# Attention beside a Fourier product on one core: the turned rows' transfers on ACT's queue, PV bursts of 6, 6 and 4 chunks, and stage two's half products added straight from PSUM by VectorE

## The chip, the cores and the metric

One core of a Trainium2 chip runs the whole program. The metric is the device time of one execution in microseconds (us); lower is better. A measurement of this kernel is the median over several executions, and one further execution is recorded by the hardware profiler. The engines are TensorE (PE; its weight loads are PEld), VectorE (DVE), ScalarE (ACT), GpSimd (POOL) and SyncE (SP), which here only issues transfers (DMAs).

## The reference

Two independent results stand side by side in the output, the left 1024 columns from attention and the right 1024 from a Fourier mix:

```python
# A: 2048 x 1024 input, 32 heads of 32 columns, one shared key and value head
q = (x @ wq).reshape(1, 2048, 32, 32).transpose(0, 2, 1, 3)
k, v = x @ wk, x @ wv
p = softmax(einsum("bhqd,bkd->bhqk", q, k) * 32 ** -0.5)
a = einsum("bhqk,bkd->bhqd", p, v)  ->  (2048, 1024) @ wo
# B: real part of a two-dimensional Fourier transform of another 2048 x 1024 input
ar = einsum("bsd,ed->bse", xb, hid_re);  ai = einsum("bsd,ed->bse", xb, hid_im)
b = einsum("ts,bse->bte", seq_re, ar) - einsum("ts,bse->bte", seq_im, ai)
out = concatenate([a, b], axis=-1)
```

## The kernel before

**Two streams on TensorE.** The first stream is attention: 32 units (a block `b` of 512 queries times a group `g` of 4 heads), each of 32 steps. A step `n` makes one scores block of 128 queries by 1024 keys (`scores`, L592, tile `pss`, two buffers in PSUM), from which VectorE takes the row maximum into `nm` (`TENSOR_REDUCE nm<-pss`) and ScalarE, one step later, the exponentials' sums (`row_sums`, L603). The same step makes, for the unit before, one block of transposed scores (`expo`, L655, tile `pst`, one buffer of two banks), whose exponentials ScalarE writes to a tile `p` (13 of these exist). Scores run 44 steps ahead of `expo` (`SU + LEAD`, 32 + 12).

The second stream is the **fill**: all other matrix products, cut into groups that add up in one PSUM bank (`psb`, two banks in all): keys, values and queries, then **stage one** and **stage two** of the Fourier mix, then the output product with `wo`. Each product is computed as three products of split operands (hi and lo: `rh`, `rl` on the right, `mh`, `ml` on the left; hi by hi, hi by lo, lo by hi), so a group of 8 right tiles has 24 matrix instructions, which this text calls 24 fills. `level` (L745) spreads the fills evenly over the steps, about five a step, and `take` (L341) issues them. `pos["fill"]` counts them, and everything that prepares operands is timed by that count.

**PV bursts.** At three steps of each unit (`ENDS`, twice the entries of `CUT`, L664: here steps 12, 22 and 32) `pv` (L666) multiplies the finished `p` tiles by the values `v`: one burst of 6, 5 and 5 chunks of 128 keys. A burst uses the psb bank that the open group does not use; `aside` (L367) first issues up to 6 fills so that a group is never within 6 fills of its start or end when a bank is borrowed. No fills are issued in a step that ends in a burst.

**Turned rows.** When all scores of a unit are done, `lse_1`, `lse_1b` and `lse_2` make, from the maxima and sums, three rows of numbers per query block. `lse_3` (L634) turns them by a transposition on TensorE into a borrowed psb bank, and VectorE copies the result to the tile `mt`. `lse_4` (L643) sends `mt` away in three transfers of 8 KB: two into rows 96 and 97 of the unit's query tile `qst`, where `expo` of that unit reads them, and one to `r_d` in DRAM. `TURN` and `LSE` (L714, L715) set the steps: counted from the first step after the unit's last scores, `lse_1` in step 1, `lse_1b` in 2, `lse_2` in 4, `lse_3` in 6, `lse_4` in 8. Step 12 of that count is the first `expo` of the unit.

**Operands of the fill.** Right operands (`RL`) and left ones (`ML`) go through four stages each: load by SP's queue into a staging tile (`r`, three buffers for the first source and two for the second; `m` likewise), `comb` (L200), which adds or subtracts the sources on GpSimd, the hi `cast` (L174, on GpSimd after the start), and `lo`, a subtraction on GpSimd. An operand is due by a fill count; a right one is loaded and combined 40 fills ahead of that, cast 14 ahead, and its lo made 8 ahead. SP issues all loads and stores of the program in one order, and a load into a staging tile waits there until GpSimd has read the tile's last contents.

**Stage two.** Seven products (`PRODUCTS`, a scheme of Strassen's kind) of 16 right tiles and 8 row blocks `k` each. The 16 right tiles make two halves of 8, so a product is two sets of 8 groups with 24 fills. Lefts of products 1, 2, 4, 5 and 6 are sums of two sources, rights of 1, 3, 5, 6 and 7 too. Each product goes to one or two output blocks `y(t, e, k)`. In the first half VectorE copies a group's bank to a tile `qh` and it is stored to `hs` in DRAM. In the second half `hs` is loaded again, VectorE adds the bank to it, and GpSimd adds that joined block to each output block that exists already (64 additions in all); a first contribution is stored as it is. Blocks that a group needs are loaded into one of six `y` tiles 24 fills before the group ends, and stored 9 fills after it ends (`BEHIND`).

Of the kernel before, what the change touches and what calls it, by code (L numbers as in the profile page):

```python
# [8 lines left out]
F32 = mybir.dt.float32  # L9
F32R = mybir.dt.float32r  # L10
AF = mybir.ActivationFunctionType
# [5 lines left out]
P = 128  # L17
S = 2048
D = 1024
H = 32  # L20
DH = 32
W = 512
# [65 lines left out]
def tile_kernel(ctx: ExitStack, tc, xT, wq, wkv, wo, xbT, wT, cT, out):  # L88
# [44 lines left out]
    def move(q, to, of):  # L133
        q.dma_start(to.bitcast(F32), of.bitcast(F32))
# [34 lines left out]
                k = next(k for k in (3, 2, 1, 0) if self.may(k))  # L169
                self.step(k)  # L170

    pos = {"fill": 0, "s": 0}

    def cast(to, of):  # L174
        if pos["fill"] < START:
            act.activation(to, of, AF.Copy)
        else:
            gp.tensor_copy(to, of)
# [19 lines left out]
            sp.dma_start(it.t[-1], a)  # L198

    def comb(it):  # L200
        if it.pre:
            return
        for t, (_, sg) in zip(it.t[1:], it.srcs[1:]):
            (gp.tensor_add if sg > 0 else gp.tensor_sub)(it.t[0], it.t[0], t)
        if it.raw is not None:
            store(it.raw[0], it.t[0], it.raw[1])
# [69 lines left out]

    prev = {"set": -200, "this": 0}
    end = [0]

    def pump():  # L280
        RL.pump()
# [25 lines left out]
    def store(to, of, key=None):  # L307
        def go():
            move(sp, to, of)
            if key:  # L310
                ready.add(key)
        soon(go)
# [28 lines left out]
    def take(n):  # L341
        for _ in range(n):
            if cur["group"] >= len(groups):
                return
            g = groups[cur["group"]]
            j = pos["fill"] - g.at
            if j == 0:
                cur["ps"] = bank("psb", True)
            if j % 3 == 0:
                RL.force(g.right[j // 3])  # L350
            if j % 12 == 0:
                ML.force(g.left[j // 12])
            product(g, cur["ps"], j)
            pos["fill"] += 1
            if j == g.n - 1:
                cur["group"] += 1
                assert all(hasattr(it, "done") for it in g.ys)
                g.post(cur["ps"])
                cur["at"] += 1
                used[cur["bank"]] = cur["at"]  # L360
                cur["bank"] = None
                if g.ys:
                    at(pos["fill"] + 2 * BEHIND, lambda n=len(g.ys): yused.__setitem__(0, yused[0] + n))
            pump()
            run_later()
# [106 lines left out]
    def have(key, ap):  # L472
        assert key in ready, key
        return ap

    def stage2():
        seen, total = {}, {}
        for _, _, outs in PRODUCTS:
            for t, e, _ in outs:
                total[t, e] = total.get((t, e), 0) + 1  # L480
        for f, (mt, nt, outs) in enumerate(PRODUCTS):
            hs = [dram.tile([P, W], F32, name=f"hs_{f}_{k}") for k in range(8)]
            for half in range(2):
                R = [Item([(lambda s=s, k=k: have((k, s), s_d[k][s]), -1 if nt == SUB and i else 1) for i, k in enumerate(nt)])
                     for s in range(half * 8, half * 8 + 8)]
                for k in range(8):
                    left = []
                    for q in range(2):
                        s0 = half * 8 + q * 4
                        left.append(Item([(lambda a=a, k=k, s0=s0: cT[a[0], a[1] * 8 + k, :, s0:s0 + 4], a[2]) for a in mt]))  # L490
                    if half == 0:
                        def post(ps, k=k, hs=hs, f=f):
                            o = op.tile([P, W], F32, name="qh")
                            dve.tensor_copy(o, ps)
                            store(hs[k], o, ("h", f, k))
                        yield Group(left, R, post)
                        continue
                    part = Item([(lambda k=k, hs=hs, f=f: have(("h", f, k), hs[k]), 1)])
                    ys = [part]
                    plan = []  # L500
                    for t, e, sg in outs:
                        n = seen.get((t, e, k), 0)
                        seen[t, e, k] = n + 1
                        it = None
                        if n:
                            it = Item([(lambda t=t, e=e, k=k: y_d[t][e][k], 1)])
                            ys.append(it)
                        r0 = (t * 8 + k) * P
                        to = out[r0:r0 + P, D + e * W:D + (e + 1) * W] if n + 1 == total[t, e] else y_d[t][e][k]
                        plan.append((sg, it, to))  # L510

                    def post(ps, part=part, plan=plan):
                        h = part.y
                        dve.tensor_add(h, h, ps)
                        for sg, it, to in plan:
                            if it is not None:
                                (gp.tensor_add if sg > 0 else gp.tensor_sub)(it.y, it.y, h)
                                store(to, it.y)
                            elif sg > 0:
                                store(to, h)  # L520
                            else:
                                o = op.tile([P, W], F32, name="qh")
                                act.activation(o, h, AF.Copy, scale=-1.0)
                                store(to, o)
                    yield Group(left, R, post, ys=ys)


# [115 lines left out]
    def lse_4(u):  # L643
        mt = lse.pop(u)
        for a in range(2):
            move(sp, qst[u][96 + a:97 + a].rearrange("o h (t c) -> o (h t) c", c=P), mt[a * NC:(a + 1) * NC])
        sp.dma_start(r_d[u], mt[2 * NC:])

    def inverse(u):
        rb[u] = onp.tile([P, W], F32, name="rb")  # L650
# [10 lines left out]
            te.matmul(ps[:, a], kst[:, c * P:(c + 1) * P], qst[u][:, 2 * hp_ + a], start=True, stop=True)  # L661
        act.activation(pt[u, c, hp_], ps, AF.Exp)

    CUT = (0, 6, 11, NC)  # L664

    def pv(u, k):  # L666

        aside()
        ps = bank("psb")
        for c in range(CUT[k], CUT[k + 1]):  # L670
            for h in range(4):
                te.matmul(ps[h * DH:(h + 1) * DH], v[:, c], pt[u, c, h // 2][:, h % 2], start=c == CUT[k], stop=c == CUT[k + 1] - 1)
        if k == 0:
            ov[u] = onp.tile([P, W], F32, name="ov")
            dve.tensor_copy(ov[u], ps)
        else:
            dve.tensor_add(ov[u], ov[u], ps)
        cur["at"] += 1
        if k == len(CUT) - 2:
            b, g = units[u]  # L680
            hi_ = onp.tile([P, W], F32R, name="oh")
            lo_ = onp.tile([P, W], F32R, name="ol")
            lse["out"] = hi_, lo_

            last = u + 1 == len(units)
            e = dve if last else gp

            def low():
                e.tensor_sub(lo_, ov[u], hi_.bitcast(F32))
                if not last:  # L690
                    store(oh_d[b][g], hi_)
                    store(ol_d[b][g], lo_, ("o", b, g))

            ends.append(lambda: e.tensor_mul(ov[u], ov[u], rb[u]))
            ends.append(lambda: e.tensor_copy(hi_, ov[u]))
            ends.append(low)

    def score_step(s):

        if s < total:  # L700
            u, r = divmod(s, SU)
            if r == SU - 6 and u + 1 < len(units):
                open_unit(u + 1)
        if SU <= s < SU * (len(units) + 1) and s % SU == TURN:
            lse_3((s - SU) // SU)
        if s < total:
            scores(s)
        row_sums(s - 1)
        u, e = divmod(s - SU, SU)
        if 0 <= u < len(units):  # L710
            for f in LSE.get(e, ()):
                f(u)

    TURN = 6  # L714
    LSE = {1: (lse_1,), 2: (lse_1b,), 4: (lse_2,), 8: (lse_4,)}  # L715

    room = [(lambda t=t, k=k: t[:, k]) for t in [pp.tile([P, 2, W], F32, name="p") for _ in range(NP)] for k in range(2)]
    for n, (it, to) in enumerate(zip(RL.items, room)):
# [7 lines left out]
    take(66)  # L726
    for s in range(SU + LEAD):
        score_step(s)
        take(7)

    PRO = pos["fill"]
# [13 lines left out]
    def level(n):  # L745
        r = n % SU
        if r in ENDS:
            return
        more = min(e for e in ENDS if e > r) - r
        left = goal(n + more) - pos["fill"]  # L750
        take(left - left * (more - 1) // more)

    for n in range(total):
        u, r = divmod(n, SU)
        if n == total - 12:
            w1 = wo_set(1)
            add([o_group(NQ - 1, t, e, ws) for e, ws in ((0, w0), (1, w1)) for t in range(4)])
        score_step(n + SU + LEAD)
        if ends:
            ends.pop(0)()  # L760
        expo(n)
        if r == 16:
            inverse(u)
        if r in ENDS and n:
            pv((n - 1) // SU, (ENDS.index(r) - 1) % (len(CUT) - 1))
        level(n)


# [70 lines left out]
```

## Time and profile before

| | us |
|---|---|
| median of 3 runs (lowest, highest) | 2813.01 (2805.11, 2813.58) |
| the profiled execution | 2811.13 |
| its span on the core | 2809.3 |
| PE busy | 2767.0 |
| ACT busy | 2176.8 |
| DVE busy | 1601.6 |
| POOL busy | 1598.2 |

The profiled execution's own time has 1.8 us outside the span. In the trace all of the kernel's own instructions carry line 66, the helper that records them, so they are told apart by their tiles' names: `out<-in`. Buffer numbers are left out, so all the `psb` banks have one name. SPq is SP's queue, which issues transfers. PE is busy nearly throughout, but its instructions are pipelined, and a busy PE can be a slow one: the granted clock stands beside it in the tables by stretch.

Counted by its matrix instructions, the fill reaches stage one at about 350 us, stage two at 1054 us and the output product at 2498 us. The halves of stage two's products begin at 1054, 1156, 1253, 1355, 1463, 1566, 1662, 1763, 1879, 1982, 2078, 2182, 2293 and 2396 us.

### The profile page before, as it was taken

The page shows a single profiled execution, that of the slowest core. Times are in us where ns is not written, and L with a number is a line of the kernel's source. Part 1 is how long each engine was busy: PE and PEld are TensorE (multiplying, and loading weights), DVE is VectorE, ACT ScalarE, POOL GpSimd, SP SyncE. Part 2 cuts the span into 40 slices and gives each one's busy share as a digit, 9 for nine tenths or more (in the row PEclk, how much of TensorE's full clock was granted, in tenths as well). Part 3 has the DMA queues.
Part 4 walks back from the last instruction along what each step waited for, and adds up shares of the span by engine and source line. Part 5 has one row for each costly group of instructions (what it writes and reads, how often), then busy time and mean ns, then how long its engine had stood idle before and what let it go on. Part 6 is the DMA issues. An engine that isn't in the chain of part 4 may idle for free.

```text
span 2809.3 us, 40359 instructions
## 1 busy us (share of the span) xinstructions
PE 2767.0 (98%) x13904; PEld 1936.5 (69%) x13904; DVE 1601.6 (57%) x1832; ACT 2176.8 (77%) x3151; POOL 1598.2 (57%) x1593
## 2 busy tenths in 40 slices
PE   8999999999999999999999999999999999999999
PEld 5876676676766766767666676667666667767666
DVE  6766666666666665555555555555555556556401
ACT  4578787888878888888878888878888778888740
POOL 3754524565536447766675575797787775540110
PEclk9999999999999999999999999999999999999999
DMA  7643325675676555665554464665565553554455
GB/s 257 196 147 113 125 87 188 218 240 181 214 241 207 165 161 186 185 184 149 167 193 133 150 188 140 195 211 173 186 201 169 177 185 105 169 175 150 123 168 170
DMA packets 320449, 489.73 MB, mean 174 GB/s; under 512 B 33978, under 2 KB 99002, under 8 KB 320186
## 3 DMA queue, kind: packets, MB, share of 16 engines
q1 hardware_dynamic: 320244, 487.15, 55.2%
q8 instruction: 110, 1.80, 0.3%
q14 instruction: 95, 0.78, 0.1%
HBM read 366.22 MB, written 119.28 MB: 173 GB/s over the span
## 4 chain that ended last, share of the span: by engine, by line
PE 89%; DMA 5%; POOL 2%; issue 2%; SPq 1%; ACT 1%; DVE 1%; POOLq 0%; ACTq 0%; DVEq 0%
PE psb L66 56%; PE pss L66 17%; PE pst L66 16%; DMA r<-s 2%; SPq L66 1%; POOL ml L66 1%; DMA qst<-mt 1%; POOL mh L66 0%; DMA p<-in_xT_dram 0%; ACT pss L66 0%; DMA m<-in_cT_dram 0%; POOL rh L66 0%; DMA r<-in_xT_dram 0%; ACT p L66 0%; DMA ql<-ql 0%
## 5 line engine op out<-in xcount | busy, mean ns | idle before, releaser
L66 DVE TENSOR_REDUCE nm<-pss 128x1 f32<-128x1024 f32 x1024 | 1252.6, 1223 | 594.6 <-PE pss L66 594.0
L66 ACT ACTIVATE p<-pst 128x1024 f32<-128x1024 f32 x1024 | 1053.4, 1029 | 487.2 <-PE pst L66 485.6
L66 ACT ACTIVATE pss<-pss,nm 128x1024 f32<-128x1024 f32 x1024 | 1112.9, 1087 | 69.0 <-DVE nm L66 66.7
L66 PE MATMUL psb<-rh,mh 128*128 128x512 f32 (+1 forms) x1852 | 730.9, 395 | 14.0 <-ACT rh L66 8.1
L66 PE MATMUL psb<-rh,ml 128*128 128x512 f32 (+1 forms) x1852 | 730.8, 395 | 6.4 <-POOL ml L66 6.4
L66 PE MATMUL psb<-rl,mh 128*128 128x512 f32 (+1 forms) x1852 | 729.2, 394 | 0.3 <-DVE rl L66 0.3
L66 PE MATMUL pst<-qst,kst 128*128 128x512 f32 x2048 | 654.4, 400 | 11.8 <-DMA qst<-mt 11.2
L66 PE MATMUL pss<-kst,qst 128*128 128x512 f32 x2048 | 654.8, 400 | 2.0 <-ACT pss L66 1.6
L66 PEld LDWEIGHTS pss<-kst,qst 128*128 128x128 f32 x2048 | 375.2, 188 | 162.8 <-issue 76.5
L66 POOL TENSOR_TENSOR ml<-m,mh 128x512 fp32r<-128x512 f32 x340 | 439.6, 1293 | 49.9 <-ACT mh L66 40.1
L66 PEld LDWEIGHTS pst<-qst,kst 128*128 128x128 f32 x2048 | 374.7, 188 | 128.8 <-ACT p L66 32.7
L66 PE MATMUL psb<-p,v 128*32 128x512 f32 x4096 | 462.5, 598 | 0.0
L66 PEld LDWEIGHTS psb<-rh,mh 128*128 128x128 f32 (+1 forms) x1852 | 346.9, 187 | 101.7 <-ACT rh L66 9.4
L66 PEld LDWEIGHTS psb<-rh,ml 128*128 128x128 f32 (+1 forms) x1852 | 346.8, 187 | 91.7 <-POOL ml L66 8.5
L66 PEld LDWEIGHTS psb<-rl,mh 128*128 128x128 f32 (+1 forms) x1852 | 346.8, 187 | 84.4 <-DVE rl L66 1.4
L66 POOL TENSOR_TENSOR r<-r,r 128x512 f32<-128x512 f32 x120 | 154.7, 1290 | 315.3 <-DMA r<-s 172.1
L66 PEld LDWEIGHTS psb<-p,v 128*32 128x32 f32 x4096 | 123.7, 110 | 286.9 <-issue 279.4
L66 POOL CAST mh<-m 128x512 fp32r<-128x512 f32 x339 | 208.3, 615 | 172.3 <-PE psb L66 155.9
L66 POOL CAST rh<-r 128x512 fp32r<-128x512 f32 x214 | 131.9, 616 | 264.2 <-PE psb L66 139.4
L66 POOL TENSOR_TENSOR rl<-r,rh 128x512 fp32r<-128x512 f32 x214 | 276.6, 1293 | 3.9
L66 POOL TENSOR_TENSOR m<-m,m 128x512 f32<-128x512 f32 x200 | 258.5, 1293 | 31.7 <-DMA m<-in_xbT_dram 19.6
L66 ACT ACTIVATION_READ_ACCUMULATOR pss<-pss,nm 128x1 f32 x1024 | 210.5, 206 | 0.0
(62 smaller groups left out, 690.5 us busy)
## 6 DMA issues: line engine op xcount, KB each, us to landing
m<-in_cT_dram SPq DMA_DIRECT2D x384, 256.0 KB
r<-s SPq DMA_DIRECT2D x192, 256.0 KB
y<-y SPq DMA_DIRECT2D x128, 256.0 KB
r<-in_wT_dram SPq DMA_DIRECT2D x88, 256.0 KB
m<-in_xbT_dram SPq DMA_DIRECT2D x88, 256.0 KB
y<-u SPq DMA_DIRECT2D x80, 256.0 KB
m<-in_wq_dram SPq DMA_DIRECT2D x64, 256.0 KB
qst<-qh SPq DMA_DIRECT2D x64, 256.0 KB
```

The costliest lines, as they stand in the source:

```text
L66: return lambda *a, **k: self.tc.keep_in_program_order(f(*a, **k))
```

## The change

1. `lse_4`'s three transfers are issued by ScalarE's queue instead of SP's. It is called from the main loop, right behind the burst, in step 4 of the count above; `lse_1`, `lse_1b`, `lse_2` and `lse_3` move to steps 0, 1, 2 and 4.
2. The bursts have 6, 6 and 4 chunks, at steps 12, 24 and 32. Step 4 of the count is step 24 of the unit then in `expo`, so the transposition, the second burst and the transfers stand in one step.
3. A new function `ahead(6)`, called in each burst, casts up to 6 right or left operands on ScalarE, if they were combined 12 or more fills earlier and a buffer is free. It finds one such operand in 42 of the 96 bursts and none in the others; all 42 are right ones, and 22 of them fall into stage two.
4. In stage two both halves do the same: for each output block VectorE adds the PSUM bank to the loaded block (or, for a first contribution, copies it with its sign), and the block is stored. The joined blocks `hs`, their 56 stores and 56 loads, and GpSimd's 64 additions are gone; VectorE's operations there go from 112 to 192, loads of output blocks from 64 to 160 and stores of output blocks from 96 to 192.

```diff
     def cast(to, of):
-        if pos["fill"] < START:
+        if pos["fill"] < START or pos["act"]:
             act.activation(to, of, AF.Copy)
         else:
             gp.tensor_copy(to, of)
...
     def comb(it):
+        it.at = pos["fill"]
...
+    def ahead(n):
+        pos["act"] = True
+        for _ in range(n):
+            lines = [x for x in (RL, ML) if x.may(2) and not x.items[x.n[2]].pre and pos["fill"] - x.items[x.n[2]].at >= 12]
+            if not lines:
+                break
+            min(lines, key=lambda x: x.items[x.n[2]].due).step(2)
+        pos["act"] = False
...
-                    if half == 0:
-                        def post(ps, k=k, hs=hs, f=f):
-                            o = op.tile([P, W], F32, name="qh")
-                            dve.tensor_copy(o, ps)
-                            store(hs[k], o, ("h", f, k))
-                        yield Group(left, R, post)
-                        continue
-                    part = Item([(lambda k=k, hs=hs, f=f: have(("h", f, k), hs[k]), 1)])
-                    ys = [part]
-                    plan = []
+                    ys, plan = [], []
...
-                    def post(ps, part=part, plan=plan):
-                        h = part.y
-                        dve.tensor_add(h, h, ps)
+                    def post(ps, plan=plan):
                         for sg, it, to in plan:
                             if it is not None:
-                                (gp.tensor_add if sg > 0 else gp.tensor_sub)(it.y, it.y, h)
-                                store(to, it.y)
-                            elif sg > 0:
-                                store(to, h)
+                                o = it.y
+                                (dve.tensor_add if sg > 0 else dve.tensor_sub)(o, o, ps)
                             else:
                                 o = op.tile([P, W], F32, name="qh")
-                                act.activation(o, h, AF.Copy, scale=-1.0)
-                                store(to, o)
+                                dve.tensor_scalar_mul(o, ps, float(sg))
+                            store(to, o)
...
     def lse_4(u):
         mt = lse.pop(u)
         for a in range(2):
-            move(sp, qst[u][96 + a:97 + a].rearrange("o h (t c) -> o (h t) c", c=P), mt[a * NC:(a + 1) * NC])
-        sp.dma_start(r_d[u], mt[2 * NC:])
+            move(act, qst[u][96 + a:97 + a].rearrange("o h (t c) -> o (h t) c", c=P), mt[a * NC:(a + 1) * NC])
+        act.dma_start(r_d[u], mt[2 * NC:])
...
-    CUT = (0, 6, 11, NC)
+    CUT = (0, 6,12, NC)
...
+        ahead(6)
...
-    TURN = 6
-    LSE = {1: (lse_1,), 2: (lse_1b,), 4: (lse_2,), 8: (lse_4,)}
+    TURN = 4
+    LSE = {0: (lse_1,), 1: (lse_1b,), 2: (lse_2,)}
...
         if r in ENDS and n:
             pv((n - 1) // SU, (ENDS.index(r) - 1) % (len(CUT) - 1))
+        if (r + LEAD) % SU == TURN and u + 1 < len(units):
+            lse_4(u + 1)
         level(n)
```

Three places show what moves. The first is SP's queue before, in the second half of product 4, where the turned rows of the 22nd unit leave: `mt` is behind loads of `m` and `y` tiles, whose staging tiles must be free first (`cT` is the Fourier matrix, `s` stage one's result).

```order
L66 DMA m_17783<-in_cT_dram 128x512
L66 DMA m_17785<-in_cT_dram 128x512
L66 DMA y_17808<-hs_6_409 128x512
L66 DMA y_17810<-y_0_6_247 128x512
L66 DMA y_17812<-y_1_6_255 128x512
L66 DMA qst_868<-mt 1x16x128 x2
L66 DMA r_150<-mt 16x128
L66 DMA r_17847<-s_7_322 128x512
```

ScalarE's queue in the changed program, for the same unit (`pss` rows are the sums of the scores, `p` rows the exponentials; `rh` is a cast that `ahead` moved here):

```order
L66 ACTIVATE pss,nm<-pss,nm 128x1024
L66 ACTIVATE p<-pst 128x1024
L66 ACTIVATE rh<-r_17662 128x512
L66 DMA qst_812<-mt 1x16x128 x2
L66 DMA r_150<-mt 16x128
L66 ACTIVATE pss,nm<-pss,nm 128x1024
```

The transfers now stand between two passes over scores, behind the cast of this burst, and no longer behind SP's loads.

The second place is TensorE at the same unit's transposition (`psb<-ident,nm`), before:

```order
L66 MATMUL psb<-ident,nm 48x128
L66 MATMUL pss<-kst,qst_1499 128x512 x2
L66 MATMUL pst<-qst_2184,kst 128x512 x2
L66 MATMUL psb<-rh,mh 128x512
L66 MATMUL psb<-rl,mh 128x512
```

and in the changed program:

```order
L66 MATMUL psb<-ident,nm 48x128
L66 MATMUL pss<-kst,qst_1443 128x512 x2
L66 MATMUL pst<-qst_2114,kst 128x512 x2
L66 MATMUL psb<-p,v 32x512 x24
L66 MATMUL pss<-kst,qst_1443 128x512 x2
```

Where fills followed the step's scores, the burst of 6 chunks now follows, and it takes the bank that the transposition has just used, or the bank of a group that closed just before.

The third place is GpSimd in the second half of product 4, one group long, before (`r_... <-r_...,r_...` and `m_...` rows add sources, `ml` and `rl` make the lo parts):

```order
L66 CAST mh<-m_17519 128x512
L66 TENSOR_TENSOR y_17546<-y_17546,y_17544 128x512
L66 TENSOR_TENSOR y_17548<-y_17548,y_17544 128x512
L66 TENSOR_TENSOR m_17585<-m_17585,m_17587 128x512
L66 TENSOR_TENSOR ml<-m_17519,mh 128x512
L66 TENSOR_TENSOR r_17727<-r_17727,r_17729 128x512
```

and in the changed program:

```order
L66 CAST mh<-m_17604 128x512
L66 TENSOR_TENSOR m_17667<-m_17667,m_17669 128x512
L66 TENSOR_TENSOR ml<-m_17604,mh 128x512
L66 TENSOR_TENSOR r_17830<-r_17830,r_17832 128x512
L66 CAST mh<-m_17667 128x512
```

The two additions to output blocks between the left operands' operations are gone.

More of the change, by code (lines that the diff above doesn't have):

```diff
@@ L170, in force @@
                 self.step(k)
-    pos = {"fill": 0, "s": 0}
+    pos = {"fill": 0, "s": 0, "act": False}
     def cast(to, of):
-        if pos["fill"] < START:
+        if pos["fill"] < START or pos["act"]:
             act.activation(to, of, AF.Copy)
@@ L480, in stage2 @@
                 total[t, e] = total.get((t, e), 0) + 1
-        for f, (mt, nt, outs) in enumerate(PRODUCTS):
-            hs = [dram.tile([P, W], F32, name=f"hs_{f}_{k}") for k in range(8)]
+        for mt, nt, outs in PRODUCTS:
             for half in range(2):
@@ L508, in stage2 @@
                         r0 = (t * 8 + k) * P
-                        to = out[r0:r0 + P, D + e * W:D + (e + 1) * W] if n + 1 == total[t, e] else y_d[t][e][k]
+                        to = out[r0:r0 + P, D + e * W:D + (e + 1) * W] if n + 1 == 2 * total[t, e] else y_d[t][e][k]
                         plan.append((sg, it, to))
-                    def post(ps, part=part, plan=plan):
-                        h = part.y
-                        dve.tensor_add(h, h, ps)
+                    def post(ps, plan=plan):
                         for sg, it, to in plan:
                             if it is not None:
-                                (gp.tensor_add if sg > 0 else gp.tensor_sub)(it.y, it.y, h)
-                                store(to, it.y)
-                            elif sg > 0:
-                                store(to, h)
+                                o = it.y
+                                (dve.tensor_add if sg > 0 else dve.tensor_sub)(o, o, ps)
                             else:
                                 o = op.tile([P, W], F32, name="qh")
-                                act.activation(o, h, AF.Copy, scale=-1.0)
-                                store(to, o)
+                                dve.tensor_scalar_mul(o, ps, float(sg))
+                            store(to, o)
                     yield Group(left, R, post, ys=ys)
@@ L728, in tile_kernel @@
         score_step(s)
+        if s == SU + TURN:
+            lse_4(0)
         take(7)
```

## The prediction

> **What bounds the kernel now.** I read the page's table of engines first, then the busy time by stretch, TensorE's waits, and the order of time around the longest of them.
>
> ```profile
> PE 2767.0 (98%) x13904; PEld 1936.5 (69%) x13904; DVE 1601.6 (57%) x1832; ACT 2176.8 (77%) x3151; POOL 1598.2 (57%) x1593
> ```
>
> TensorE does the same instructions before and after, and is busy 98% of the span. Work taken from GpSimd is worth nothing by itself; only TensorE's waits, and time in which it runs slowly, can be won. Where these are shows in stage two's half products, which all have 192 fills: the second halves of products 2 and 4, both halves of 5 and 6, with one left out.
>
> ```profile
> core 0: us, PE busy (x) PEld busy (x) DVE busy (x) ACT busy (x) POOL busy (x), PEclk, DMA share, GB/s
> 1354.70:1463.10 108.40, 103.78 (x523) 70.76 (x522) 58.27 (x63) 84.34 (x122) 83.96 (x82) 0.98 0.61 197
> 1763.50:1878.90 115.40, 106.82 (x523) 72.46 (x522) 58.45 (x63) 84.23 (x122) 94.94 (x91) 0.96 0.66 214
> 1878.90:1981.80 102.90, 102.90 (x535) 71.74 (x534) 58.76 (x64) 85.59 (x125) 84.80 (x83) 1.00 0.55 172
> 2078.30:2182.20 103.90, 102.30 (x523) 70.03 (x522) 59.09 (x73) 83.69 (x123) 83.26 (x82) 1.00 0.54 170
> 2182.20:2292.90 110.70, 104.11 (x522) 71.88 (x521) 58.34 (x63) 84.09 (x122) 83.94 (x82) 0.97 0.57 179
> ```
>
> The same work takes 102.9 us where TensorE never waits and 115.4, 110.7 and 108.4 us in three second halves: 12.5 + 7.8 + 5.5 = 25.8 us over the undisturbed one. The waits of TensorE over all of stage two say what they are:
>
> ```profile
> PE pst L66 <- DMA qst<-mt: 11.2, 5, 4.4
> PE psb L66 <- POOL ml L66: 6.4, 4, 2.3
> PE psb L66 <- POOL mh L66: 3.5, 2, 1.9
> ```
>
> That is 21.1 us: 11.2 for the turned rows, 9.9 for left operands that GpSimd had not finished. TensorE is also slow behind these waits; the granted clock (next to last but two in a row) falls:
>
> ```profile
> 1446.00:1450.00 4.00, 4.00 (x19) 1.13 (x23) 0.69 (x1) 2.12 (x3) 2.82 (x3) 0.57 0.66 221
> 1826.00:1830.00 4.00, 4.00 (x14) 3.15 (x13) 1.60 (x4) 1.74 (x2) 4.00 (x5) 0.68 0.61 186
> 1860.00:1864.00 4.00, 4.00 (x17) 1.75 (x21) 0.69 (x1) 2.12 (x3) 3.22 (x4) 0.50 0.83 250
> 1864.00:1868.00 4.00, 4.00 (x32) 1.03 (x28) 0.00 (x0) 0.00 (x0) 4.00 (x4) 0.73 0.38 119
> 2244.00:2248.00 4.00, 4.00 (x10) 3.13 (x11) 1.60 (x4) 1.10 (x2) 4.00 (x4) 0.50 0.64 165
> ```
>
> Four us at a share c of the clock lose 4 x (1 - c): 1.7 + 1.3 + 2.0 + 1.1 + 2.0 = 8.1 us. Waits and slow time make 29.2 us, near the 25.8 of three halves, so little else is lost in this stage.
>
> The Trainium skill ("TensorE: Matmul & The Clock Gate", Part 1) states that the clock halves after an idle window of about 3.4 us and comes back after about as long busy; the 0.50 behind the 4.4 us wait agrees. By that, each of four gaps would cost an estimated 1.7 us, 6.8 in all, against 8.1 from the rows.
>
> **The turned rows.** The longest wait, in order of time on VectorE, SP's queue and TensorE:
>
> ```profile
> 1842.28 0.28 DVE L66 COPY mt<-psb 48x128 f32<-48x128 f32 x1 [0.51 <-PE psb L66]
> ...
> 1846.99 0.43 SPq L66 DMA_DIRECT2D out_dram<-y  x1
> 1852.14 0.81 SPq L66 DMA_DIRECT2D m<-in_cT_dram  x2
> ...
> 1854.46 1.16 SPq L66 DMA_DIRECT2D qst<-mt  x2
> ...
> 1859.85 1.19 PE L66 MATMUL pst<-qst,kst 128*128 128x512 f32 x2 [4.40 <-DMA qst<-mt]
> SPq L66 <- POOL ml L66: 899.5, 245, 14.9
> ```
>
> `mt` is ready at 1842.6, its transfer is issued 11.9 us later, since SP stands on a load whose staging tile GpSimd still reads (the last row: 899.5 us of such waiting), and TensorE starts 5.4 us after that issue. In the change the transfers leave ScalarE in the burst of step 24, eight steps ahead of the use at step 32. 1024 steps in the span of 2809 us, less some 150 ahead of the first, are 2.6 us each, so eight are about 20 us, against 5.4. **Gain: 11.2 us of waits and the slow time behind two of them, 1.7 + 2.0 + 1.1 = 4.8.** SP loses 96 issues of about 0.6 us and gains 80 others of 0.43, which nobody waits for at that length.
>
> The Trainium skill speaks against this ("DMA: Bandwidth & Descriptors", section "Issuing engines are not separate DMA queues"): whichever engine starts them, transfers share the same 16 DMA engines, and only issue time is saved. The trace agrees that 5.4 us remain behind the issue, and shows 11.9 us ahead of it.
>
> **GpSimd's additions.** The stretch before the wait at 1822 us, on GpSimd, and its waits in the halves 4b (second of product 4) and 5a:
>
> ```profile
> 1808.63 2.55 POOL L66 TENSOR_TENSOR y<-y,y 128x512 f32<-128x512 f32 x2
> 1811.13 1.29 POOL L66 TENSOR_TENSOR m<-m,m 128x512 f32<-128x512 f32 x1
> 1812.37 1.30 POOL L66 TENSOR_TENSOR ml<-m,mh 128x512 fp32r<-128x512 f32 x1
> 1820.42 1.27 POOL L66 TENSOR_TENSOR r<-r,r 128x512 f32<-128x512 f32 x1 [6.75 <-DMA r<-s]
> ...
> POOL r L66 <- DMA r<-s: 20.2, 6, 6.8
> POOL r L66 <- DMA r<-s: 11.5, 6, 3.6
> L66 POOL TENSOR_TENSOR y<-y,y 128x512 f32<-128x512 f32 x64 | 82.0, 1293 | 61.4 <-DVE y L66 41.9 <-PE pst L66 17.4 <-DMA m<-in_cT_dram 2.2
> L66 DVE TENSOR_TENSOR y<-y,psb 128x512 f32<-128x512 f32 x168 | 113.1, 681 | 33.7 <-PE psb L66 27.1 <-DMA y<-y 2.9 <-DMA r<-s 0.9
> L66 POOL CAST rh<-r 128x512 fp32r<-128x512 f32 x214 | 131.9, 616 | 264.2 <-PE psb L66 139.4 <-DMA r<-in_wo_dram 42.0 <-PE pst L66 38.3
> L66 ACT ACTIVATE rh<-r 128x512 fp32r<-128x512 f32 x8 | 5.1, 632 | 7.2 <-DMA r<-in_xT_dram 7.1
> ```
>
> It is a ring: GpSimd is late with `ml`, so SP issues the loads of `m` late and, behind them, those of `r`; GpSimd then idles 6.75 us for `r`, and is later still. Half 4b has 16 additions, 16 x 1.29 = 20.7 us on top of what half 5a does, where sums of two lefts and of two rights are made just as well; 5a, and 6a, have no addition, and in 5a TensorE waits for nothing. After the change all second halves have GpSimd's load of first ones, less 22 casts of 0.616 us in the stage. **Gain: 9.9 us of waits and 1.3 + 2.0 = 3.3 of slow time.**
>
> VectorE's 80 further operations are 80 x 0.68 = 54 us in the stage's 1444 us; it is busy 58.8 of 102.9 in half 5a, so 3.9 more on average fit. Where a first contribution is made twice in one group (first half of product 1, 8 groups), both `qh` buffers are used at once, and a group must find its predecessor's stored. The nearest case is `ql`, one buffer, with the same 24 fills between uses:
>
> ```profile
> DVE ql L66 <- DMA ql<-ql: 4.6, 4, 2.2
> PE psb L66 <- DVE ql L66: 1.6, 2, 1.0
> ```
>
> 31 such groups cost TensorE 1.6 us; 8 cost between 0 and, at 1.0 each, 8; I take 1.
>
> **What ScalarE gets.** In a burst it idles for the next transposed scores (its waits for them, then one burst of 5 chunks):
>
> ```profile
> ACT p L66 <- PE pst L66: 485.6, 285, 6.6
> 1836.83 1.03 ACT L66 ACTIVATE p<-pst 128x1024 f32<-128x1024 f32 x1 [4.13 <-PE pst L66]
> ```
>
> A cast of 0.63 us and the three transfers, 1.16 + 0.57 = 1.73 us by SP's rows, make 2.4 and fit into 4.1; a sixth chunk lengthens the burst. Cover gone, 31 x 1.73 = 54 us would be the price. A cast can wait for GpSimd's sum: nothing, or the 6.75 us above, for 22 casts in the stage. Since GpSimd is late less often, I take 2 us in all. Twelve steps between the first and second burst instead of ten repeat what the first twelve do already: nothing.
>
> **The burst behind the transposition.** TensorE's rows at the same unit:
>
> ```profile
> 1841.97 0.27 PE L66 MATMUL psb<-ident,nm 128*48 128x128 f32 x1
> ...
> 1843.01 0.39 PE L66 MATMUL psb<-rh,mh 128*128 128x512 f32 x1
> ```
>
> The burst can start where the fill starts now, 1.04 us after the transposition; it needs the bank. The copy of `mt` ends at 1842.56, 0.59 us after. If a group closed just before, VectorE has one or two additions of 0.68 us ahead: 1.27 or 1.95. So a burst waits between 0 and 0.91 us, 28 us over 31 units at most. A borrowed bank's group is 6 fills away as a rule, and where the group has just closed the burst takes the other bank: I take 2 us.
>
> **Sum:** 11.2 + 4.8 + 9.9 + 3.3 = 29.2 won, 1 + 2 + 2 = 5 lost: 24 us off the profiled execution's 2811.1 is 2787. The median of the runs is 1.9 above that execution, so against it I say **2788 us**.
>
> **The rivals.**
> - *The ring stays.* SP still waits for GpSimd, `r` comes late, and every first half now loads output blocks through SP too. For it: 11.5 us of waiting for `r` in 5a. Against: TensorE's empty list there. The 13.2 us stay: 2801. Chance 0.17.
> - *The turned rows stay late,* since the transfer and not its issue is slow, as the rule on DMA engines would have it. For it: 5.4 us behind the issue. Against: 20 us of room. 16 us stay: 2804. Chance 0.08.
> - *The burst waits for the copy* with two additions ahead of it in most units: 0.91 x 31 - 2 = 26 more, 2814, no change. For it: stage two's products 1 to 4 and 7 make two additions a group. Against: at this unit VectorE idled 0.51 us ahead of the copy. Chance 0.10.
> - *ScalarE is held, and it is slower.* A cast stands in order behind GpSimd's sum; behind it wait the transfers, the sums of scores and the next exponentials, and TensorE has one `pst` buffer. Its length by this row:
>
> ```profile
> POOL r L66 <- DMA r<-s: 172.1, 59, 12.6
> ```
>
>   A sum is late by 2.9 us on average, 12.6 at most. A cast that waits 6.75 us costs 6.75 + 2.4 - 4.1 = 5 us; from 1.5 us for each of the 22 casts it is slower by more than a measurement's doubt (33 us). With 11 of 22 at 5 us, 55 are lost: 2843. Against: 16 fills lie between sum and cast. Chance 0.12.
>
> **How the numbers follow.** My forecast has 0.53, with its own range of 2778 to 2799: 29 us won and nothing lost is 2784, and the runs shown spread over 8.5 us, so 6 more are left below; above, 11 us for the costs that I took too low. A measurement tells about 0.3%, 8.4 us, from no change: faster is below 2804.6, slower above 2821.4. The forecast gives faster 0.52; the ring 0.10 of its 0.17; late rows 0.04 of 0.08: 0.66. Slower: 0.12 and 0.02 of the third rival: 0.14. The rest, 0.20, is no change. For 8 in 10 the range reaches from 2776 over the rivals to 2814.
>
> **What would show it.** Right: no TensorE wait for `qst<-mt`, none of over 1 us for `ml` and `mh`, half 4b near 103 us and a granted clock of 1.00 in it; ScalarE's idle time before `p` smaller by about 2 us in one burst of three. Wrong: a wait of the first PV instruction for `mt` or `y`; gaps of ScalarE before `rh<-r`; GpSimd's waits for `r<-s` as long as before; or waits for VectorE's `qh` around 1054 to 1156 us.

## The result, and the profile after

The changed kernel is slower: 2834.56 us (median of 4 runs, 2831.18 to 2838.66) against 2810.17 (4 runs, 2805.11 to 2813.58), a ratio of 1.0089, 95% interval 1.0066 to 1.0112. Forecast were 2788 us and a range of 2776 to 2814; both are missed, on the other side of no change.

The changed kernel's page, its span and table of engines:

```profile
span 2836.8 us, 40625 instructions
PE 2773.8 (98%) x13904; PEld 1943.5 (69%) x13904; DVE 1643.2 (58%) x1912; ACT 2197.9 (77%) x3193; POOL 1496.4 (53%) x1487
```

The work moved as the diff says: GpSimd loses 102 us of busy time, VectorE gains 42, ScalarE 21. None of that is the 27.5 us by which the span grew. Some of TensorE's rows of waits (us in all, times, longest) name it:

```profile
PE pss L66 <- ACT pss L66: 36.8, 10, 6.5
PE psb L66 <- POOL ml L66: 2.9, 2, 1.7
PE psb L66 <- DVE y L66: 2.1, 6, 0.5
PE pst L66 <- ACT p L66: 1.3, 6, 0.4
```

The waits that the change was to remove are gone or smaller: none for `qst<-mt` (11.2 before), none for `mh` (3.5), 2.9 for `ml` (6.4). In their place stands one row of 36.8 us, 33.7 of them in stage two: a `pss` buffer that ScalarE has not yet read. The second half of product 4, and a stretch behind one of the longest new waits (the columns as in the prediction's tables by stretch):

```profile
1777.90:1890.50 112.60, 104.04 (x515) 71.21 (x514) 62.45 (x70) 84.60 (x124) 76.57 (x75) 0.97 0.62 203
1859.00:1863.00 4.00, 3.91 (x9) 2.94 (x10) 1.23 (x1) 3.78 (x6) 4.00 (x5) 0.50 0.07 21
```

It still takes 112.6 us (115.4 before, 103 forecast), and behind the new wait the granted clock falls to 0.50, as it did behind the old ones. Before, the new row had this length:

```profile
PE pss L66 <- ACT pss L66: 1.6, 1, 1.6
```

The sum closes: these waits make 41.8 us (36.8 + 2.9 + 2.1) where those of before make 22.7 (11.2 + 6.4 + 3.5 + 1.6), 19.1 more (all of TensorE's rows together: 57.3 against 37.9, 19.4 more); the mean clock is 0.993 of 2836.8 us against 0.996 of 2809.3, so slow time grows from about 11 to 20 us, 9 more. Together 28 us, for 27.5 measured.

**What holds ScalarE.** Its waits in the changed kernel, five rows of a pass over scores (`pss`) that waits for a transfer, and the casts' row:

```profile
ACT pss L66 <- DMA qst<-mt: 52.3, 12, 10.9
ACT pss L66 <- DMA m<-in_cT_dram: 15.7, 2, 8.9
ACT pss L66 <- DMA out_dram<-y: 10.1, 2, 9.1
ACT pss L66 <- DMA r<-s: 10.1, 1, 10.1
ACT pss L66 <- DMA y<-y: 9.3, 4, 2.8
ACT rh L66 <- POOL r L66: 5.8, 4, 2.2
```

The casts hardly wait. The pass over scores behind the transfers waits 97.5 us in 21 waits, 45.2 of them for transfers (`m`, `out_dram`, `r<-s`, `y`) that ScalarE never issued and whose data this pass doesn't read. (The name is the one that the profile infers; a row named `qst<-mt` can be a wait for another transfer too, as the 22nd unit shows below.) ScalarE's order of time at the 22nd unit (ACTq rows are transfers that it issues), and TensorE's behind it:

```profile
1846.05 0.53 ACTq L66 DMA_DIRECT2D qst<-mt  x1
1846.14 0.19 ACT L66 ACTIVATION_READ_ACCUMULATOR pss<-pss,nm 128x1 f32 x1
1846.23 1.01 ACT L66 ACTIVATE p<-pst 128x1024 f32<-128x1024 f32 x1
1847.14 0.63 ACT L66 ACTIVATE rh<-r 128x512 fp32r<-128x512 f32 x1
1854.32 0.51 ACTq L66 DMA_DIRECT2D qst<-mt  x1
1857.41 0.32 ACTq L66 DMA_DIRECT2D r<-mt  x1
1857.84 1.09 ACT L66 ACTIVATE pss<-pss,nm 128x1024 f32<-128x1024 f32 x1 [10.07 <-DMA qst<-mt]
...
1859.09 1.22 PE L66 MATMUL pss<-kst,qst 128*128 128x512 f32 x2 [5.94 <-ACT pss L66]
```

The first transfer leaves at 1846.05, so the data are there. The second, of the same tile and with nothing more to wait for in the kernel, leaves 8.3 us later, the third 3.1 us after that. The chain of waits says what the third waited for (start, length, what):

```profile
1848.28 1.28 POOL ml L66
1849.56 0.02 issue
1849.58 0.33 SPq L66
1849.91 0.05 issue
1849.96 0.42 SPq L66
...
1851.43 0.38 SPq L66
1851.81 0.04 issue
1851.85 5.54 DMA r<-s
1857.39 0.02 issue
1857.41 0.32 ACTq L66
...
1857.84 0.10 ACT pss L66
...
1859.09 1.22 PE pss L66 x2
```

A load of `r` that SP issued lands at 1857.39, and 0.02 us later ScalarE's third transfer leaves. In the same way the second left at 1854.32, 0.02 us after the landing of a load of `m` that SP had issued at 1849.96. These loads and ScalarE's transfers share no data. What they share is seen in the built program, and in the trace's record of each transfer: every transfer of SP and of ScalarE signals its landing on one of eight semaphores, given in turn over both queues together, and waits first until the transfer that had the same one before has landed. Around this unit, in the order of numbering:

```
engine  transfer              signals   waits first for
SP      m_17718 <- cT         0         0, GpSimd
SP      m_17720 <- cT         1         1
SP      y_17750, y_17752      2, 3      2, 3
ACT     qst <- mt (1st)       4         4, VectorE
SP      r_17830 <- s          5         5, ScalarE
SP      r_17832 <- s          6         6
SP      m_17835, m_17837      7, 0      7, 0 (GpSimd)
ACT     qst <- mt (2nd)       1         1  = SP's m_17720
SP      out blocks, m         2 .. 5    ...
ACT     r_150 <- mt (3rd)     6         6  = SP's r_17832
```

SP stood on the first of these two loads of `m` until GpSimd's `ml` ended at 1849.56 and freed its staging tile; `m_17720` was issued at 1849.96, and `r_17832` stood behind it in SP's order. So ScalarE stands behind SP, and SP behind GpSimd: the engine that reads TensorE's scores has been tied to the ring that the prediction described for GpSimd and SP.

The trace keeps the semaphore of every transfer and the landings on it, so all 96 transfers can be checked. 31 of them left within 0.1 us of the landing of the transfer that had used their semaphore last, and ScalarE stood about 77 us in all ahead of these 31 (from the end of the record before on ScalarE to the issue). Ahead of the other 65 it stood over 0.5 us only once, 0.77. In 28 of the 31 that earlier transfer is SP's; in three, ahead of stage two, the third transfer waits for ScalarE's own first. It is mostly the second and the third that stand, but not only: at 2112, 2197 and 2281 us the first does (2.9, 1.2 and 4.9 us).

### The profile page after: what moved, and what is told of

It reads as the page before. It is cut to its first block, busy times and chain, and to the rows that moved or that the text cites. A ratio compares the mean times of both kernels' runs of the same rounds, so it can differ in the third digit from the quotient of the medians.

```text
span 2836.8 us, 40625 instructions
## 1 busy us (share of the span) xinstructions
PE 2773.8 (98%) x13904; PEld 1943.5 (69%) x13904; DVE 1643.2 (58%) x1912; ACT 2197.9 (77%) x3193; POOL 1496.4 (53%) x1487
## 4 chain that ended last, share of the span: by engine, by line
PE 82%; DMA 6%; POOL 3%; issue 3%; ACT 2%; DVE 2%; SPq 1%; ACTq 0%; POOLq 0%; DVEq 0%
PE psb L66 52%; PE pss L66 16%; PE pst L66 15%; DMA r<-s 3%; DMA m<-in_cT_dram 1%; POOL ml L66 1%; ACT pss L66 1%; SPq L66 1%; DVE nm L66 1%; ACT p L66 1%; POOL mh L66 1%; DVE y L66 0%; DMA ql<-ql 0%; POOL rh L66 0%; DMA p<-in_xT_dram 0%
## 5 line engine op out<-in xcount | busy, mean ns | idle before, releaser
L66 PE MATMUL pss<-kst,qst 128*128 128x512 f32 x2048 | 659.1, 403 | 36.8 <-ACT pss L66 36.8
L66 POOL TENSOR_TENSOR r<-r,r 128x512 f32<-128x512 f32 x120 | 154.7, 1289 | 367.2 <-DMA r<-s 200.6
L66 POOL CAST rh<-r 128x512 fp32r<-128x512 f32 x172 | 106.1, 617 | 241.1 <-PE psb L66 149.4
```

The source lines that it names most:

```text
L66: return lambda *a, **k: self.tc.keep_in_program_order(f(*a, **k))
```

## The experiments

The theory, S: the second and third transfer hold ScalarE through the shared semaphores. Rivals: the casts hold it, the new stage two does, or any issue on ScalarE does. Each kernel ran beside the kernel before on one chip; the ratio is to that.

**1. The transfers back on SP, all else as changed.**

```diff
-            move(act, qst[u][96 + a:97 + a]...
-        act.dma_start(r_d[u], mt[2 * NC:])
+            move(sp, qst[u][96 + a:97 + a]...
+        sp.dma_start(r_d[u], mt[2 * NC:])
```

> The changed kernel with one thing undone: lse_4's three transfers are issued by SP's queue again, at the new place behind the second burst. Theory S (ScalarE's queue stands still at the second and third transfer, because each transfer waits for the landing of an earlier one of SP's that used the same completion semaphore, and SP stands behind GpSimd): TensorE's waits for ACT's pss (36.8 us in the changed kernel) fall below 5 us, qst<-mt may come up to 12 us late but has 20 us of room, so no wait for it; 2785 to 2800 us. Theory C (the casts that ahead puts on ScalarE hold it): at least 2825 us, the waits for ACT's pss stay over 25 us. Theory L (the added loads and stores of output blocks through SP make operands late): at least 2820 us.

2797.93 us (5 runs), ratio 0.9961 (0.9944 to 0.9979). Its TensorE waits:

```profile
PE psb L66 <- POOL ml L66: 4.9, 4, 1.7
PE psb L66 <- DVE y L66: 3.9, 7, 1.6
...
PE pss L66 <- ACT pss L66: 1.9, 3, 1.1
...
PE psb L66 <- POOL mh L66: 1.4, 2, 0.8
```

36.8 us of waiting have become 1.9, and 37 us of time are gone (2834.56 to 2797.93, measured on two occasions; by the ratios 1.0089 and 0.9961, 36). The queue alone turns a small gain into a loss.

**2. The kernel before with only the transfers on ScalarE, at their old place.** The converse edit of `lse_4` alone.

> The kernel before with one thing of the change: lse_4's three transfers on ScalarE's queue, at their old place (step 8 of the count, no burst beside it). Theory S: ScalarE stands for 2 to 12 us in most units of stage two with no burst to cover it; TensorE waits 40 to 100 us for ACT's pss; 2840 to 2890 us. Theories C and L: the turned rows' waits of 11 us go and nothing comes in their place but 2 us of issuing per unit; 2795 to 2815 us.

2944.89 us, ratio 1.0491 (1.0475 to 1.0507): the direction was right, the size far over what S had been given. TensorE's longest wait, ScalarE's longest ones for transfers, and SP's wait for GpSimd:

```profile
PE pst L66 <- ACT p L66: 115.1, 29, 14.0
...
ACT p L66 <- DMA m<-in_cT_dram: 53.5, 6, 14.4
ACT p L66 <- DMA y<-hs: 26.3, 3, 9.9
...
SPq L66 <- POOL ml L66: 1027.6, 250, 19.3
```

At this place it is the exponentials that stand behind the transfers, and TensorE has one `pst` buffer where it has two of `pss`: 29 waits of up to 14 us. By the same count as above ScalarE stands about 103 us ahead of its transfers, where it stood 77 in the changed kernel, so the larger part of the difference lies in what stands behind them. SP's wait for GpSimd grows from 899.5 to 1027.6; that the lateness feeds back, which my estimate had left out, would fit this, but no run separates it.

**3. The changed kernel without `ahead(6)`; 4. the changed kernel with the old stage two.**

```diff
-        ahead(6)
```

> The changed kernel without the call of ahead: all casts on GpSimd as before. Theory S: 2825 to 2845 us, ScalarE's gaps behind the transfers stay. Theory C: 2785 to 2805 us.

> The changed kernel with stage two as before (half products stored, loaded, joined by VectorE, added by GpSimd). Theory S: ScalarE still stands, and for longer since GpSimd is later: 2835 to 2865 us, waits for ACT's pss 35 us or more. Theory L: 2795 to 2815 us.

2831.64, ratio 1.0088 (1.0072 to 1.0105), and 2831.41, ratio 1.0081 (1.0064 to 1.0098). Both keep the slowdown, with 28.9 and 28.7 us of waits for `pss <- ACT pss`; with the old stage two S had expected somewhat more of both, 2835 us and 35. Neither the casts nor the new stage two are its cause.

**5. Only the first of the three transfers on ScalarE.**

```diff
-            move(act, qst[u][96 + a:97 + a]...
-        act.dma_start(r_d[u], mt[2 * NC:])
+            move(act if a == 0 else sp, qst[u][96 + a:97 + a]...
+        sp.dma_start(r_d[u], mt[2 * NC:])
```

> The changed kernel with only the first of the three transfers on ScalarE's queue, the other two on SP's. Theory S (ScalarE stands because the second and third transfer were given completion semaphores last used by loads of SP that come late; the first never was): ScalarE stands nowhere, waits for ACT's pss below 5 us, 2794 to 2804 us. Rival Q (a transfer on ScalarE's queue costs by itself, whatever semaphore it has): about a third of the loss stays, 2808 to 2815 us.

2796.46, ratio 0.9962 (0.9948 to 0.9977), 3.7 us of waits for `pss <- ACT pss`. A transfer issued by ScalarE costs next to nothing where the semaphore's last user has landed. It hadn't always: ahead of three of the 32 first transfers ScalarE still stood (2.1, 5.7 and 0.6 us, at 1916, 2082 and 2159), each time until 0.1 us after the landing of a load by SP. So the expectation that it stands nowhere was not met, and the first transfer is less exposed, not free.

**6. All three on GpSimd's queue, whose transfers signal on semaphores of their own.** `gp` in place of `act` in `lse_4`.

> The changed kernel with lse_4's three transfers on GpSimd's queue, whose transfers complete on semaphores of their own. Theory S (a transfer first waits until the one that had its completion semaphore before has landed, and SP's and ScalarE's share eight): no sums of scores held behind the transfers, PE's waits for sums of scores under 5 us, 2794 to 2806, and GpSimd may wait a little for mt. Rival (any transfer of mt that is issued in that step, by whichever engine but SP, holds its engine for 5 to 10 us, because the data or the ring for it is late): GpSimd stands 5 us or more in a unit, 2815 or more.

2796.59, ratio 0.9956 (0.9942 to 0.997), 2.0 us of waits for `pss <- ACT pss`. TensorE's waits for `ml` and `mh` are 5.9 us, against 6.3 in experiment 1. GpSimd does stand, though for VectorE's copy of `mt` and not for SP's transfers, and without a cost that shows in the time:

```profile
POOL qst L66 <- DVE mt L66: 131.6, 19, 32.6
```

The rival (lateness of the data holds whoever issues) expected 2815 or more and falls. With 1, 2 and 5, and the landings counted above, this settles S.

That leaves the gain. With the transfers off ScalarE the change wins 10 us by the runs (2808.36 to 2797.93) and 13.1 by the profiled spans (2809.3 to 2796.2), where 24 were forecast. The spans flatter: the profiled execution of the kernel before took 2811.1 us, where the medians beside these experiments are 2805 to 2808.

**7. The kernel before with the new stage two alone; 8. experiment 1 with the old stage two; 9. experiment 1 without the casts.**

> The kernel before with only stage two's new half products. By the prediction's second term the waits for GpSimd's ml and mh (9.9 us) and 3.3 us of slow time go: 2795 to 2800 us. If the ring of SP and GpSimd stays, since every half now loads and stores output blocks through SP: 2804 to 2812 us, ml and mh above 5 us.

> The changed kernel with the transfers on SP's queue and stage two as before, so that the earlier turned rows, the bursts and the casts stand alone. By the prediction's first term (16 us less 2 to 4 for bursts and casts): 2794 to 2800 us and no wait for qst<-mt. If SP issues them too late here as well: 2803 to 2812 us.

> The changed kernel with the transfers on SP's queue and without ahead. If the casts cost ScalarE more than they give GpSimd: 2790 to 2795 us; if they help GpSimd: 2800 to 2806 us; theory S itself says nothing of it, and within 3 us of 2798 is no difference.

2798.83, ratio 0.9974 (0.9962 to 0.9985); 2794.34, ratio 0.9958 (0.9945 to 0.9971); 2802.13, ratio 0.9981 (0.9972 to 0.999). TensorE's waits with the new stage two alone:

```profile
PE pst L66 <- DMA qst<-mt: 7.8, 4, 3.0
...
PE psb L66 <- DVE y L66: 1.5, 4, 0.4
...
PE psb L66 <- POOL ml L66: 0.4, 2, 0.2
```

and with the early turned rows, the bursts of 6, 6 and 4 and the casts on the old stage two:

```profile
PE psb L66 <- POOL ml L66: 9.0, 7, 1.7
...
PE psb L66 <- POOL mh L66: 1.6, 1, 1.6
```

Each term does its own work: the new stage two takes the waits for `ml` and `mh` from 9.9 to 0.4, the early rows take that for `qst<-mt` from 11.2 to nothing. But they don't add: 7 (2805.34 - 2798.83) and 11 us (2805.34 - 2794.34) alone, 10 together (by the profiled spans 14.5, 17.4 and 13.1), where `ml` and `mh` are back at 6.3 us. In ratios, 0.26% and 0.42% would make 0.9932; 0.9961 was measured, 0.0029 more, with an uncertainty of about 0.0025 (the root of the sum of the three intervals' squared half widths), so only just outside it.

**10. The kernel before with the new stage two and earlier rows on SP, bursts left at 6, 5, 5; 11. the same with the casts.**

```diff
-    TURN = 6
-    LSE = {1: (lse_1,), 2: (lse_1b,), 4: (lse_2,), 8: (lse_4,)}
+    TURN = 4
+    LSE = {0: (lse_1,), 1: (lse_1b,), 2: (lse_2,), 5: (lse_4,)}
```

> The kernel before with the new stage two and the turned rows made two steps earlier and sent two steps earlier (TURN 4, lse_4 in step 5 of the count instead of 8) on SP's queue, bursts left at 6, 5, 5, no casts in bursts. If the two gains add up as the prediction had it and only the bursts' new form ate some: the new stage two alone ran in 2798.8 and left 7.8 us of waits of TensorE for qst<-mt; these go, with some 3 us of slow time, so 2785 to 2793, no qst<-mt wait, ml and mh under 2 us together, waits for DVE y under 2. Rival (the early rows themselves push SP's loads back, so that ml and mh come late again): 2796 or more with ml and mh at 4 us or more.

> c_early with the casts in the bursts. With the transfers on SP the casts brought 4 us (2797.9 against 2802.1, the intervals of the ratios just apart). If they help by taking work from GpSimd where it is late: 2 to 4 us under c_early. If GpSimd is no longer late there, within 2 us of c_early.

2802.06 (11 runs), ratio 0.998 (0.9971 to 0.9989), and 2795.69, ratio 0.9958 (0.9945 to 0.997). Experiment 10 is no faster than the new stage two alone, as its rival had it. Its row for `ml`, and SP's wait for the copy `mt`:

```profile
PE psb L66 <- POOL ml L66: 10.0, 7, 2.3
...
SPq L66 <- DVE mt L66: 157.7, 25, 11.8
```

SP waited for `mt` 20.6 us in experiment 7, 25.7 before. Put earlier in SP's order, the transfers now come before their data, and SP stands on them with the loads of `m` and `r` behind. The casts bring 6 us here (2802.06 to 2795.69, the intervals just apart), more than the 2 to 4 expected; the 4 us between experiments 9 and 1 lie within intervals that overlap, other than my expectation of 11 said.

**12. Experiment 11 with `lse_4` one step later.**

```diff
-    LSE = {0: (lse_1,), 1: (lse_1b,), 2: (lse_2,), 5: (lse_4,)}
+    LSE = {0: (lse_1,), 1: (lse_1b,), 2: (lse_2,), 6: (lse_4,)}
```

> c_early_cast with lse_4 in step 6 of the count instead of 5, so two steps behind the transposition as in the kernel before, where SP stood only 25.7 us in all for VectorE's copy mt (17 times). In c_early SP stood 157.7 us (25 times, up to 11.8) with the loads of m and r behind, and TensorE's waits for ml came to 10.0 us. If that standing is what feeds the lateness of ml back: SP's wait for mt falls to 20 to 50 us, ml and mh to 3 us or less, no qst<-mt wait above 1 us, and the time is 2786 to 2793, under the 2795.7 of c_early_cast. Rival (ml is late there for another reason, such as the order of loads as a whole): ml stays at 4 us or more and the time within 3 us of 2795.7.

2794.5 (5 runs, 2787.37 to 2795.48), ratio 0.9959 (0.9946 to 0.9973). SP's wait for `mt` falls from 154.8 to 92.8 us, not to 20 to 50, `ml` from 5.6 to 4.0 and `mh` from 1.2 to nothing; the median lies within 3 us of experiment 11's, as the rival had it. All three fall together, but the time doesn't tell the two apart. It stays open how much of `ml`'s lateness SP's standing for `mt` makes. Against it: the long stands of experiment 10 in stage two (the longest are 11.5 us ahead of 1592 and 11.8 ahead of 2413) are not right in front of TensorE's waits for `ml`. In experiment 6, too, SP stands only 4.7 us for `mt`, against 98.5 in experiment 1, and TensorE waits as long for `ml` and `mh`; but there GpSimd itself stands for `mt`. Experiments 1, 5, 6, 8, 11 and 12, at ratios of 0.9956 to 0.9962, are alike within what these runs can tell.

## Why the prediction was wrong

**The step that failed** is the one on ScalarE: "A cast of 0.63 us and the three transfers, 1.16 + 0.57 = 1.73 us by SP's rows, make 2.4 and fit into 4.1". The issues themselves were sized well: 0.53, 0.51 and 0.32 us at the 22nd unit. What was not asked is what each transfer waits for before it is issued. I took `mt` to be all of it. They wait, the second and third above all, for transfers of SP as well, so where 1.73 us had been counted, a pass over scores waited up to 10.9 behind them. The built program names these semaphores with each transfer, so this could have been read beforehand: three transfers, numbered among loads that SP issues late. Experiments 1, 5 and 6 show it by removing it in three ways. Of the 49 us between 24 won and 24 lost (2810.17 to 2834.56), this step makes about 37; the rest is the gain, which came to 10 instead of 24.

**The rival of a held ScalarE** had the right chain (sums of scores behind it, then TensorE) and the right side, 2843 against 2834.56, at a chance of 0.12. It named the casts as what holds it; they waited 5.8 us in all, and experiment 3 without them is as slow. Its objection, 16 fills between sum and cast, was right, and kept me from seeing that the same chain had a second entry. That its time came near the measured one is luck: it was added up from a cause that wasn't at work.

**The turned rows:** right. They are on time in every form that sends them earlier, and most of the 16 us (11.2 and 4.8) came with the old stage two: 11 us by the runs, 17.4 by the profiled spans (2809.3 to 2791.9), bursts and casts included. The rival that they stay late falls. The Trainium skill ("DMA: Bandwidth & Descriptors", section "Issuing engines are not separate DMA queues") says that issuing from several engines saves only the issuing engine's time. Here even that was dearly bought: SP got rid of 96 issues, and ScalarE stood up to 10.9 us for three.

**GpSimd's additions and the ring:** right in what they remove, too large in sum. Alone the new stage two brings 7 us by the runs (4 to 11 by the interval) where 13.2 were forecast, though the waits for `ml` and `mh` went as said. The rival that the ring stays is right in one thing, a sign that the prediction had named: GpSimd's waits for `r<-s` did not shorten (172.1 us before, 191.7 with the new stage two alone, 200.6 in the changed kernel). TensorE's waits for `ml` fell all the same. The half that was to take 103 us takes 105.5 there, with the longest wait for `qst<-mt`, 3.0 us, still in it:

```profile
1765.70:1871.20 105.50, 102.26 (x523) 70.37 (x522) 62.93 (x71) 83.47 (x122) 74.00 (x73) 1.00 0.64 209
```

In experiment 1 it takes 103.1, but the first half of product 5, undisturbed at 102.9 before, takes 104.4:

```profile
1764.80:1867.90 103.10, 101.61 (x514) 70.00 (x513) 62.48 (x71) 84.64 (x124) 72.35 (x70) 1.00 0.63 210
1867.90:1972.30 104.40, 103.37 (x534) 71.50 (x533) 59.18 (x65) 86.80 (x127) 82.94 (x81) 1.00 0.60 195
```

In the second row TensorE idles 1.0 us (104.40 less 103.37), which it did not before.

**The sum** took the two terms as independent. They are not: together they bring no more than one of them. What joins them is not shown. Of the move of the turned rows the prediction asked whether the data come in time for the reader, 20 us, and not whether the transfer now comes too early for the queue that issues it. On SP it does (98.5 us of standing for `mt` in experiment 1, 25.7 before), but experiments 6 and 12 don't show that this is what costs. The sum's last step is also off by one: 2811.1 less 24.2, and 1.9 more, is 2789 and not 2788.

**The small costs:** `qh` buffers 1 us forecast, none seen in stage two. The burst behind the transposition 2 us; TensorE's products never wait for `mt` (13 weight loads do, 0.5 us at most), and its waits for `DVE y` (2.1 in the changed kernel, 3.9 in experiment 1) are of that size. So the rival that the burst waits for the copy falls. The casts, for which the prediction had no gain of their own in its sum, bring 6 us in experiment 11, about as much as the new stage two does alone.

## What to carry to other kernels

Before a transfer is put on an engine that computes, list all that it waits for, its completion semaphore's last user included: an engine that issues in order inherits the lateness of whoever shares the semaphore, and everything behind it on that engine is late too. A sign of it in a trace is a wait of a computing engine for a transfer whose data it doesn't read. Here three transfers were worse than one, since the later ones are numbered behind the other queue's loads. And two gains that touch the same queues need not add; the combination is costed as a case of its own, a step moved earlier also against the queue that then stands on it.

## What was not expected of the hardware

The page of the changed kernel lists ScalarE's transfers as a queue of their own:

```profile
q10 hardware_dynamic: 3072, 0.79, 0.1%
```

A separate queue, 0.1% of the DMA engines' time, and still tied: the eight semaphores that the program shares out over both bind it to SP's queue, so a 0.5 us issue cost a pause of 10.07 us, while GpSimd's queue, with semaphores of its own, showed none of it (experiment 6). Unexpected too was how much depends on the place: the same three transfers cost 37 us ahead of a sum of scores with two `pss` buffers, and 137 us (2944.89 against 2808.36) ahead of exponentials with one `pst` buffer. The two kernels differ in the bursts beside the transfers, the casts and stage two as well; the old stage two at the new place also loses about 35 us by the ratios (1.0081 against 0.9958), but no run separates the buffers from the burst.
